# Loading two weight matrices and one V block in halves, summing P times V on DVE, in a decode kernel of one core

## The chip, the cores and the metric

The kernel runs on one core of a Trainium2 chip. The metric is the device time of one execution in microseconds (us), as the median of several runs. TensorE is PE (PEld loads its weights), VectorE is DVE, ScalarE is ACT, GpSimd is POOL; SyncE is SP and issues nearly all DMAs.

## The reference

Two branches over the same input x (2 batches, one position, D = 1024) are mixed by a gate. Branch A is attention with one new query per batch over a cache of 16,384 positions in 32 heads of 128; branch B is an MLP mixer with four weight matrices. All in bfloat16:

```python
x = A_x
g = _sigmoid((x * gate_w).sum(-1, keepdims=True))
# A:
q = (x @ wq).reshape(B, Sq, H, Dh).transpose(0, 2, 1, 3)
scores = jnp.einsum("bhqd,bhkd->bhqk", q, k_cache) * (Dh ** -0.5)
p = _softmax(scores, axis=-1)
o = jnp.einsum("bhqk,bhkd->bhqd", p, v_cache)
a = o.transpose(0, 2, 1, 3).reshape(B, Sq, H * Dh) @ wo
# B: (the shifts of h by positions give zeros, as there is one position)
h = _gelu(_layernorm(x) @ w1);  x1 = x + shifted(h) @ w2
b = x1 + _gelu(_layernorm(x1) @ w3) @ w4
out = g * a + (1 - g) * b
```

K and V are 268 MB each; w3 and w4 7.3 MB each, wq and wo 8.4 MB each, w1 and w2 2.1 MB each. Every byte is used once.

## The kernel before, in words

The work is cut into 32 units. A unit u is a pair of heads (hp, 16 of them) and a batch b; its K and its V are 8.4 MB each, 64 KB to a partition. SBUF holds one large buffer, `mem`, of five cells of 32 KB a partition. K takes cells 0 and 1 in even units, 1 and 2 in odd ones; V takes cells 3 and 4, but the last unit but one has its V in cells 0 and 1. Before the units, cells 3 and 4 hold wq, then w3, then w4, one after the other, and cell 2 holds w1 and w2. So what SP may load next is set by who still reads the cells.

All loads go through SP's queue, in the order of the program; an issue that has to wait holds all that stand behind it. The order before: wq, x, gate_w, w1, w2, K0, w3 (once the q projection has read wq), K1, the first four heads of wo, w4 (`LinearT.load`, L210, once the w3 matmuls have read w3), K2, V0 (`load_v`, L100, once the w4 matmuls have read w4), and then in turn K and V.

In unit n, `score_first` transposes four of eight chunks of K on DVE (L425, two buffers `KT`) and multiplies them on PE with the query (L431). This frees the cell that the next K needs, and `load_k(n + 1)` (L97) is issued. `score_second` does the other four. `softmax_a` and `softmax_b` take the maximum of all scores (the product of `Dm`, L462; DVE's `nb`, L468), the exponentials on ACT (L470) and the sum of their rows (L481, L483). `pv(n - 2)` multiplies the exponentials of two units earlier with their V (L503) into an `oacc` of 128 rows by four blocks of 128 columns; then `load_v(n - 1)` is issued. `pv_end(n - 2)` brings the sum: `pv_sum` copies `oacc` with a scale on ACT (L516), four fp32 products with columns of the selecting matrix `sel8` (L521) add up the blocks, and DVE scales the result by the gate into `OT` (L533). After the second batch of a pair `wo_project` adds the pair's output to two rows of 512 columns, `arow` (L404), in two column groups of PE.

In units 0 and 1 the MLP fills the place of `pv`: `lin3.compute` in unit 0 (a quarter of the w3 matmuls, `softmax_b`, the other three quarters, all at L217), `lin4.compute` in unit 1 in the same way, then `mlp_post4`, which writes branch B into `arow` (L379). wo comes in tiles of four heads (`load_wo`, L397, one buffer).

In the last unit V comes in eleven pieces (`PIECES`, L108), so that `pv_last` can follow them: three pieces as in `pv`, the others with V as the stationary operand (L548). wo's last two heads are loaded behind them. Then DVE and ACT each copy one half of the output row (L606, L608), and SP and ACT store them.

Of the kernel before, what the change touches and what calls it, by code (L numbers as in the profile page):

```python
# [10 lines left out]
FP32 = mybir.dt.float32  # L11
BF16 = mybir.dt.bfloat16
ACTF = mybir.ActivationFunctionType
ALU = mybir.AluOpType
# [9 lines left out]
def kernel(  # L24
# [51 lines left out]
    def misc_psum(shape, dtype=FP32):  # L76
        return mps.tile(shape, dtype, tag="misc", name="misc")
# [4 lines left out]
    def region(cell, elements):  # L82
        return mem[:, cell * CELL : cell * CELL + elements]
# [6 lines left out]
    def cache_rows(cache, u):  # L90
        hp, b = units[u]
        return cache[b, 2 * hp : 2 * hp + 2].rearrange("h s d -> (h s) d").rearrange(
            "(p j) d -> p (j d)", p=P
        )
# [4 lines left out]
    def load_v(u):  # L99
        nc.sync.dma_start(out=region(v_cell[u], NJ * Dh), in_=cache_rows(A_v_cache, u))  # L100

    PIECES = [32] * 6 + [16] * 3 + [8] * 2
    assert sum(PIECES) == NJ

    def load_v_pieces(u):
# [33 lines left out]
    for v in range(4):  # L139
# [36 lines left out]
        axis=AX.X,  # L176
        op=ALU.add,
    )
    oacc = [ops.tile([P, 4 * Dh], FP32, name=f"oacc{k}") for k in range(2)]
    for k in range(2):  # L180
        nc.vector.memset(oacc[k][:], 0.0)
# [14 lines left out]

    class LinearT:

        def __init__(self, W, actT, name, cell, offset):
            self.actT = actT  # L200
            K, self.N = W.shape
            self.R = K // P
            self.C = self.N // P
            self.src = W.rearrange("(p r) n -> p (r n)", p=P)
            at = cell * CELL + offset
            self.dst = mem[:, at : at + self.R * self.N]
            self.acc = mlp.tile([P, self.C, B], FP32, name=f"{name}_acc")

        def load(self):
            nc.sync.dma_start(out=self.dst, in_=self.src)  # L210

        def compute(self, c0, c1):
            wc = self.dst.rearrange("p (r n) -> p r n", n=self.N)
            ps = misc_psum([P, c1 - c0, B])
            for c in range(c0, c1):
                for r in range(self.R):
                    nc.tensor.matmul(  # L217
                        ps[:, c - c0, :],
                        lhsT=wc[:, r, :].rearrange("p (m c) -> p c m", c=self.C)[:, c, :],
                        rhs=self.actT[:, r, :],  # L220
                        start=(r == 0),
                        stop=(r == self.R - 1),
                    )
            nc.vector.tensor_copy(out=self.acc[:, c0:c1, :], in_=ps[:])  # L224

    xn1T = mlp.tile([P, KC, B], BF16)
    hT = mlp.tile([P, KC, B], BF16)
# [5 lines left out]

    lin1 = LinearT(B_w1, xn1T, "w1", 2, 0)
    lin2 = LinearT(B_w2, shT, "w2", 2, KC * D)
    lin3 = LinearT(B_w3, xn2T, "w3", 3, 0)
    lin4 = LinearT(B_w4, h2T, "w4", 3, 0)
    lin1.load()
    lin2.load()
    load_k(0)  # L240
# [5 lines left out]
    for h in range(H):  # L246
        for r in range(KC):
# [4 lines left out]
                start=(r == 0),  # L252
                stop=(r == KC - 1),
            )
    lin3.load()
    qT = const.tile([P, H, B], BF16)
    nc.vector.tensor_copy(out=qT[:], in_=qps[:])
    qdps = misc_psum([P, 4, H * B])
# [100 lines left out]
        nc.vector.tensor_tensor(out=x1T[:], in0=lin2.acc[:], in1=xT[:], op=ALU.add)  # L359
        layernorm_T(x1T[:], xn2T[:], "ln2")  # L360

    NH2 = D // 512
    arow_t = [rps.tile([QP * k + B, 512], FP32, name=f"arow{k}") for k in range(NH2)]
    arow = [arow_t[k][QP * k : QP * k + B, :] for k in range(NH2)]

    def mlp_post4():

        omg = mlp.tile([P, B], FP32, name="omg")
        nc.vector.tensor_scalar(
            out=omg[:], in0=g_rep[:], scalar1=-1.0, scalar2=1.0, op0=ALU.mult, op1=ALU.add  # L370
        )
        nc.vector.tensor_tensor(out=bT[:], in0=lin4.acc[:], in1=x1T[:], op=ALU.add)
        nc.vector.tensor_tensor(
            out=bT[:], in0=bT[:], in1=omg[:].unsqueeze(1).to_broadcast([P, KC, B]), op=ALU.mult
        )
        W = 512 // KC
        for k in range(NH2):
            for c in range(KC):
                nc.tensor.matmul(  # L379
                    arow[k].rearrange("b (m c) -> b c m", c=KC)[:, c, :],  # L380
                    lhsT=bT[:, c, :],
                    rhs=ident_f[:, k * W : (k + 1) * W],
                    start=(c == 0),
                    stop=False,
                    skip_group_check=True,
                )

    OT = const.tile([P, H, B], BF16)
    WOH = 4
    wo_view = A_wo.rearrange("(h d) n -> d h n", d=Dh)  # L390
    wo_tiles = {}

    def load_wo(h0, n, step=WOH):
        t = wopool.tile([P, WOH, D], BF16, name="wo")
        for k in range(0, n, step):
            z = min(n, k + step)
            nc.sync.dma_start(out=t[:, k:z, :], in_=wo_view[:, h0 + k : h0 + z, :])  # L397
        for k in range(n):
            wo_tiles[h0 + k] = t[:, k, :]

    def wo_project(hp):
        for h in (2 * hp, 2 * hp + 1):
            for k in range(NH2):
                nc.tensor.matmul(  # L404
                    arow[k],
                    lhsT=OT[:, h, :],
                    rhs=wo_tiles[h][:, k * 512 : (k + 1) * 512],
                    start=False,
                    stop=(h == H - 1),
                    skip_group_check=True,  # L410
                )

    S_tiles = {}
    st_tiles = {}
# [44 lines left out]
    def softmax_b(u):  # L459
# [9 lines left out]
        for e, rows in enumerate(halves):  # L469
# [6 lines left out]
                accum_out=rs[rows],  # L476
            )
        rs_tiles[u] = rs
        tot_ps = misc_psum([P, 2])
        if u < NU - 1:  # L480
            nc.tensor.matmul(tot_ps[:, 0:1], lhsT=lmat[:], rhs=rs[:], start=True, stop=True)  # L481
# [29 lines left out]
    def pv(u):  # L511
        pv_moving(u, 0, NJ // 4, NJ // 4)

    def pv_sum(u, ot, scaled, last):
        osb = ppool.tile([P, 4 * Dh], FP32, name="osb")
        nc.scalar.activation(  # L516
            out=osb[:], in_=oacc[u % 2][:], func=ACTF.Copy,
            scale=rinvs[u % NP][:, 0:1] if scaled else 1.0,
        )
        for k in range(4):  # L520
            nc.tensor.matmul(  # L521
                ot[:],
                lhsT=osb[:, k * Dh : (k + 1) * Dh],
                rhs=sel8[:, k : k + 5 : 4],
                start=(k == 0),
                stop=(last and k == 3),
            )

    def pv_end(u):
        hp, b = units[u]  # L530
        ot = misc_psum([P, 2])
        pv_sum(u, ot, True, True)
        nc.vector.tensor_scalar(  # L533
            out=OT[:, 2 * hp : 2 * hp + 2, b], in0=ot[:], scalar1=g_rep[:, b : b + 1],
            scalar2=None, op0=ALU.mult,
        )
        if b == B - 1:
            wo_project(hp)

    def pv_last(u):  # L540
        hp, b = units[u]
        ot = misc_psum([P, 2])
        moving = sum(PIECES[:3]) // 4
        pv_moving(u, 0, moving, moving)
        pv_sum(u, ot, False, False)
        V = v_view(u)
        for j in range(4 * moving, NJ):
            nc.tensor.matmul(  # L548
                ot[:],
                lhsT=V[:, j, :],  # L550
                rhs=pts[u % NP][:, j // 4, :, j % 4],
                start=False,
                stop=(j == NJ - 1),
            )
        nc.vector.tensor_tensor(
            out=OT[:, 2 * hp : 2 * hp + 2, b], in0=ot[:], in1=rinvs[u % NP][:], op=ALU.mult
        )
        wo_project(hp)

    compute_gate()  # L560
    layernorm_T(xT[:], xn1T[:], "ln1")
    lin1.compute(0, lin1.C)
    mlp_post1()
    lin2.compute(0, lin2.C)
    mlp_post2()

    for n in range(NU):
        score_first(n)
        if n + 1 < NU:
            load_k(n + 1)  # L570
        else:
            load_v(NU - 2)
        score_second(n)
        softmax_a(n)
        if n == 0:
            lin3.compute(0, FC // 4)
            softmax_b(n)
            lin3.compute(FC // 4, FC)
            gelu_T(lin3.acc[:], h2T[:], FC)
            load_wo(0, WOH)  # L580
            lin4.load()
        elif n == 1:
            lin4.compute(0, KC // 4)
            softmax_b(n)
            lin4.compute(KC // 4, KC)
            mlp_post4()
            load_v(0)
        else:
            pv(n - 2)
            if n < NU - 1:  # L590
                load_v(n - 1)
            else:
                load_v_pieces(NU - 1)
            pv_end(n - 2)
            if n == NU - 1:
                load_wo(H - 2, 2, 1)
            softmax_b(n)
        if n % 4 == 1 and n > 1:
            load_wo(n - 1, min(WOH, H - 2 - (n - 1)))
    pv(NU - 2)  # L600
    pv_end(NU - 2)
    pv_last(NU - 1)

    out_row = mlp.tile([QP + B, 512], BF16)
    rows = out.rearrange("b s d -> (b s) d")
    nc.vector.tensor_copy(out=out_row[0:B, :], in_=arow[0])  # L606
    nc.sync.dma_start(out=rows[:, 0:512], in_=out_row[0:B, :])
    nc.scalar.activation(out=out_row[QP : QP + B, :], in_=arow[1], func=ACTF.Copy)  # L608
    nc.scalar.dma_start(out=rows[:, 512:1024], in_=out_row[QP : QP + B, :])


# [28 lines left out]
```

## Time and profile before

| | |
|---|---|
| median of 3 runs | 1347.13 us (1347.13 to 1348.85) |
| the profiled execution | 1348.32 us; its span, from the first to the last instruction, 1346.6 us |
| mean granted TensorE clock | 0.781 |
| busy: PE, PEld, DVE, ACT, POOL | 790.9, 367.0, 644.4, 127.1, 15.2 us |
| DMA | 573.33 MB, 426 GB/s over the span |
| packets of SP's queue | 16052, 572.54 MB |
| first and last K landing of the units (transposes of unit 3 and unit 31 start) | 177.26 and 1281.67 us |

Times in the profile are microseconds from the start of the span. A line of the timeline gives the start, the time it took, the engine, the line of the kernel, the operation, what it writes and reads, how many instructions it merges, and, in brackets, how long the engine had been idle and what ended that. "SPq L97" is a DMA issue by SP from line 97. A window's line gives the busy time of each engine with the number of instructions, the granted clock, the share of 16 DMA engines in use, and GB/s.

### The profile page before, as it was taken

To read this page: it belongs to the slowest core of one execution; us is meant where nothing else is said; L and a number is where in the kernel's file an instruction comes from. 1 tells how busy PE (TensorE), PEld (TensorE's weight loads), DVE (VectorE), ACT (ScalarE), POOL (GpSimd) and SP (SyncE) were. 2 spreads that over 40 slices of the span, in tenths; PEclk is the share of its full clock that TensorE was granted. 3 is DMA by queue.
4 is the path that set the end of the run, shared out by engine and by line. 5 is a ranking of instruction groups with operands and counts; after the bars stand their busy time and mean duration, and the time that the engine had idled before them with its cause. 6 is when DMAs were issued, how large, how long until landed. Compare 5 with 4: busy or idle time off the path is not lost.

```text
span 1346.6 us, 12381 instructions
## 1 busy us (share of the span) xinstructions
PE 790.9 (59%) x5542; PEld 367.0 (27%) x5542; DVE 644.4 (48%) x503; ACT 127.1 (9%) x197; POOL 15.2 (1%) x54
## 2 busy tenths in 40 slices
PE   2678765554766545566555556655456664555665
PEld 2455322222222222222222222222222222222222
DVE  0434555444555534455554345555344555444450
ACT  0010101111110011110011111001111100111110
POOL 1000000000000000000000000000000000000000
PEclk9967877777887667888777788777778876777886
DMA  9988999999999999999999999999999999999997
GB/s 406 432 368 387 435 436 427 425 429 437 433 431 433 428 439 435 433 433 425 433 433 435 435 435 435 435 432 426 437 437 425 429 433 437 433 433 429 435 435 303
DMA packets 16109, 573.33 MB, mean 426 GB/s; under 512 B 1844, under 2 KB 1848, under 8 KB 6584
## 3 DMA queue, kind: packets, MB, share of 16 engines
q1 hardware_dynamic: 16052, 572.54, 98.8%
q8 instruction: 43, 0.70, 0.2%
q14 instruction: 10, 0.08, 0.0%
q10 hardware_dynamic: 4, 0.00, 0.0%
HBM read 572.53 MB, written 0.00 MB: 425 GB/s over the span
## 4 chain that ended last, share of the span: by engine, by line
DMA 66%; PE 16%; DVE 12%; issue 4%; ACT 0%; another core or an unknown queue 0%; POOL 0%; SPq 0%; DVEq 0%; ACTq 0%
DMA mem<-in_A_k_cache_dram 62%; PE S L431 12%; DVE KT L425 12%; DMA mem<-in_A_v_cache_dram 3%; PE misc L217 3%; DMA xin<-in_A_x_dram 2%; PE misc L248 1%; ACT pt L470 0%; PE arow L379 0%; PE oacc L503 0%; POOL ln_rstd L329 0%; PE misc L462 0%; PE arow L404 0%; PE misc L481 0%
## 5 line engine op out<-in xcount | busy, mean ns | idle before, releaser
L431 PE MATMUL S<-KT,qw 128*128 128x512 bf16 x2048 | 547.9, 418 | 388.4 <-DVE KT L425 388.2
L425 DVE STREAM_TRANSPOSE KT<-mem 128x2048 f32<-128x2048 f32 x256 | 570.8, 2282 | 297.3 <-DMA mem<-in_A_k_cache_dram 245.8
L431 PEld LDWEIGHTS <-qw 128*128 128x128 bf16 x2048 | 219.0, 107 | 712.2 <-issue 533.8
L503 PE MATMUL oacc<-mem,pt 128*8 128x512 bf16 x2008 | 116.9, 386 | 8.7 <-DMA mem<-in_A_v_cache_dram 8.7
L456 ACT ACTIVATE Dm<-ident_s,m 128x128 f32<-128x128 f32 x32 | 12.9, 402 | 1018.4 <-DVE m L454 1018.4
L470 ACT ACTIVATE pt<-St,nb 64x256 bf16<-64x256 f32 x64 | 89.7, 1401 | 58.4 <-DVE nb L468 57.5
L533 DVE TENSOR_SCALAR OT<-misc,g_rep 128x2 bf16<-128x2 f32 x31 | 6.9, 222 | 143.5 <-PE misc L521 143.5
L481 PE MATMUL misc<-rs,lmat 128*128 128x1 f32 x62 | 18.2, 362 | 90.0 <-ACT pt L470 90.0
L503 PEld LDWEIGHTS <-pt 128*8 128x8 bf16 x2008 | 46.7, 87 | 75.7 <-issue 25.3
L452 DVE STREAM_TRANSPOSE St<-S 128x512 f32<-128x512 f32 x32 | 22.9, 717 | 66.2 <-PE S L431 66.2
L483 DVE RECIPROCAL rinv<-misc 128x1 f32<-128x1 f32 x31 | 5.2, 169 | 102.2 <-PE misc L481 102.2
L521 PE MATMUL misc<-sel,osb 128*128 128x2 f32 x256 | 33.7, 254 | 27.1 <-ACT osb L516 27.1
L481 PEld LDWEIGHTS misc<-rs,lmat 128*128 128x128 f32 x62 | 15.5, 311 | 101.2 <-ACT pt L470 101.2
L521 PEld LDWEIGHTS misc<-sel,osb 128*128 128x128 f32 x256 | 31.0, 191 | 43.3 <-ACT osb L516 43.3
L217 PEld LDWEIGHTS <-mem 128*128 128x128 bf16 x576 | 36.3, 170 | 1.8 <-issue 1.4
L470 ACT ACTIVATION_READ_ACCUMULATOR pt<-St,nb 64x1 f32 x64 | 30.5, 477 | 0.0
L516 ACT ACTIVATE osb<-oacc,rinv 128x512 f32<-128x512 f32 x31 | 21.3, 687 | 72.6 <-PE oacc L503 72.6
L248 PE MATMUL misc<-xT,mem 128*128 128x2 bf16 x256 | 7.1, 165 | 26.1 <-DVE xT L243 23.3
L280 POOL TENSOR_TENSOR qw<-qd,mask 128x16 bf16<-128x16 bf16 x32 | 8.4, 265 | 1195.2 <-PE S L431 1166.6
L468 DVE TENSOR_REDUCE nb<-misc 64x1 f32<-64x64 f32 x64 | 14.2, 222 | 5.3 <-PE misc L462 1.3
L224 DVE COPY w_acc<-misc 128x16 f32<-128x16 f32 (+4 forms) x6 | 1.1, 176 | 31.4 <-PE misc L217 31.4
L462 PE MATMUL misc<-Dm,ones_f 128*128 128x128 f32 x64 | 15.8, 331 | 0.0
(83 smaller groups left out, 124.3 us busy)
## 6 DMA issues: line engine op xcount, KB each, us to landing
mem<-in_B_w_dram SPq DMA_DIRECT2D x2, 7168.0 KB, 29.1
wo<-in_A_wo_dram SPq DMA_DIRECT2D x7, 1024.0 KB, 33.0
mem<-in_A_v_cache_dram SPq DMA_DIRECT2D x6, 1024.0 KB, 24.1
mem<-in_B_w_dram SPq DMA_DIRECT2D x2, 2048.0 KB
mem<-in_A_v_cache_dram SPq DMA_DIRECT2D x3, 512.0 KB, 16.7
mem<-in_A_k_cache_dram SPq DMA_DIRECT2D x32, 28.3
wo<-in_A_wo_dram SPq DMA_DIRECT2D x1, 512.0 KB, 32.0
mem<-in_A_v_cache_dram SPq DMA_DIRECT2D x2, 256.0 KB, 13.3
```

The source lines that it names most:

```text
L217: nc.tensor.matmul(ps[:, c - c0, :], lhsT=wc[:, r, :].rearrange("p (m c) -> p c m", c=self.C)[:, c, :], rhs=self.actT[:, r, :], start=(r = ...
L248: nc.tensor.matmul(qps[:, h, :], lhsT=wq_t[:, r, h * Dh : (h + 1) * Dh], rhs=xT[:, r, :], start=(r == 0), stop=(r == KC - 1),)
L425: nc.vector.transpose(out=kt[:], in_=Kc.rearrange("p j d -> p (j d)").bitcast(FP32))
L431: nc.tensor.matmul(S, lhsT=t[:, v, NG - 1 - m : NG - 1 - m + P], rhs=ktb[:, half * GT : (half + 1) * GT, w, :, e], start=(first and n == 0 ...
L452: nc.vector.transpose(out=st[:].rearrange("p j r -> p (j r)"), in_=S[:])
L462: nc.tensor.matmul(R_ps[:], lhsT=ones_f[:], rhs=Dm[:], start=True, stop=True)
L468: nc.vector.tensor_reduce(out=nb[rows], in_=R_ps[rows, rows], axis=AX.X, op=ALU.min)
L470: nc.scalar.activation(out=Pt[rows, :, e, :].rearrange("p (m a) k -> p a k m", a=GT // 4), in_=st[rows, :, 0:NG].rearrange("p (a k) m -> p ...
L481: nc.tensor.matmul(tot_ps[:, 0:1], lhsT=lmat[:], rhs=rs[:], start=True, stop=True)
L503: nc.tensor.matmul(acc[QP * q : QP * q + 8, :], lhsT=pts[u % NP][:, g].rearrange("p h k -> p (h k)"), rhs=v_view(u)[:, 4 * g : 4 * g + 4, ...
L516: nc.scalar.activation(out=osb[:], in_=oacc[u % 2][:], func=ACTF.Copy, scale=rinvs[u % NP][:, 0:1] if scaled else 1.0,)
L521: nc.tensor.matmul(ot[:], lhsT=osb[:, k * Dh : (k + 1) * Dh], rhs=sel8[:, k : k + 5 : 4], start=(k == 0), stop=(last and k == 3),)
```

## The change

- w3, w4 and V0 are loaded in two halves each. The half k of w3 and w4 (four of eight rows of w3 to a partition, 14 of 28 of w4) goes to the start of cell 3 + k; V0's halves are the cells 3 and 4 themselves. `compute(k, c0, c1)` multiplies one half, and the second half is added to the first by DVE. The loads stand right behind the matmuls that free their cells.
- `softmax_b` is cut: the sum of the rows becomes `softmax_c`. In units 0 and 1 `softmax_b` stands in the middle of the first half's matmuls and `softmax_c` behind them.
- `pv_sum` is gone. `pv_rows` adds the four blocks of `oacc` on DVE with a mask that holds the scale and the gate; one or two fp32 products with `hsel` and two small copies give `OT`.
- `arow` is one tile of four rows groups of 256 columns at partitions 0, 32, 64 and 96, for four column groups of PE, in `mlp_post4` as in `wo_project`.
- wo is loaded by pairs of head pairs, with two neighbouring rows to a partition (4 KB runs instead of 2 KB), for 28 heads. The last four heads come as four loads of 2 KB runs behind the last V, and both last pairs are projected at the end; before, two heads came in unit 29 and two behind the last V.
- V of the last unit comes in nine pieces, seven of 32 rows and two of 16, instead of six of 32, three of 16 and two of 8.
- Four tiny loads follow `load_v` in each of units 28, 29 and 30: k rows of 10 + k elements for k of 1 to 10, 12 and 14, from gate_w into tiles that nothing reads.
- At the end DVE and ACT each convert one half of the columns of all rows, and the two batches are stored by SP and ACT.

```diff
+    def load_v_half(u, k):
+        at = slice(k * CELL, (k + 1) * CELL)
+        nc.sync.dma_start(out=region(v_cell[u], NJ * Dh)[:, at], in_=cache_rows(A_v_cache, u)[:, at])
-    PIECES = [32] * 6 + [16] * 3 + [8] * 2
+    PIECES = [32] * 7 + [16] * 2
...
+            self.at = [(cell + k) * CELL + offset for k in range(nparts)]
...
+        def load(self, k=0):
+            n = self.rows * self.N
+            nc.sync.dma_start(out=self.part(k), in_=self.src[:, k * n : (k + 1) * n])
+            if k == 0:
+                nc.vector.tensor_copy(out=acc, in_=ps[:])
+            else:
+                nc.vector.tensor_tensor(out=acc, in0=acc, in1=ps[:], op=ALU.add)
...
+    wo_pairs = A_wo.rearrange("(hp p r) n -> p hp (r n)", p=P, r=2)
+    def load_wo_last():
+        t = wo_tile(HP - LASTP)
+        for k in range(2):
+            for r in range(2):
+                nc.sync.dma_start(out=t[:, k, r, :], in_=wo_heads[:, H - 4 + 2 * k + r, :])
     def wo_project(hp):
+        for r in range(2):
+            for k in range(Q4):
                 nc.tensor.matmul(
                     arow[k],
+                    lhsT=OT[:, hp, r, :],
+                    rhs=wo_tiles[hp, r][:, k * NQ : (k + 1) * NQ],
...
+    probe_sets = {NU - 4: (2, 3, 4, 5), NU - 3: (6, 7, 8, 10), NU - 2: (12, 14, 1, 9)}
+    def load_probes(n):
+        for k in probe_sets.get(n, ()):
+            t = const.tile([k, 32], BF16, name=f"probe{k}")
+            w = 10 + k
+            nc.sync.dma_start(
+                out=t[:, 0:w], in_=gate_w[0 : k * 64].rearrange("(p f) -> p f", p=k)[:, 0:w]
+            )
...
+    def pv_rows(u, mask):
+        nc.vector.tensor_scalar(
+            out=part[:], in0=acc[:, 0:Dh], scalar1=mask[:, 0:1], scalar2=None, op0=ALU.mult
+        )
+        for k in range(1, 4):
+            in0 = acc[:, k * Dh : (k + 1) * Dh]
+            twice = k == 3
+            nc.vector.scalar_tensor_tensor(
+                out=red[:] if twice else part[:],
...
         if n == 0:
-            lin3.compute(0, FC // 4)
+            load_wo_pair(0)
+            lin3.compute(0, 0, FC // 2)
             softmax_b(n)
-            lin3.compute(FC // 4, FC)
+            lin3.compute(0, FC // 2, FC)
+            lin4.load(0)
+            softmax_c(n)
+            lin3.compute(1, 0, FC)
+            lin4.load(1)
             gelu_T(lin3.acc[:], h2T[:], FC)
-            load_wo(0, WOH)
-            lin4.load()
         elif n == 1:
-            lin4.compute(0, KC // 4)
+            lin4.compute(0, 0, KC // 2)
             softmax_b(n)
-            lin4.compute(KC // 4, KC)
+            lin4.compute(0, KC // 2, KC)
+            load_v_half(0, 0)
+            softmax_c(n)
+            lin4.compute(1, 0, KC)
+            load_v_half(0, 1)
             mlp_post4()
-            load_v(0)
         else:
             pv(n - 2)
             if n < NU - 1:
                 load_v(n - 1)
+                load_probes(n)
```

## The prediction

> **What bounds the kernel now.** I read the page's slices first, then the stream of transfers in the stretches where the slices sag, then the queue SP in the order of time, and last a middle unit and the tail. The slices (40 of 33.7 us each):
>
> ```profile
> DMA  9988999999999999999999999999999999999997
> GB/s 406 432 368 387 435 436 427 425 429 437 433 431 433 428 439 435 433 433 425 433 433 435 435 435 435 435 432 426 437 437 425 429 433 437 433 433 429 435 435 303
> ```
>
> DMA is full from end to end; no compute engine is over 59% busy. Over 177 to 1281 us the windows give 433 GB/s: that is the ceiling of this kernel, and 573 MB must pass under it. So time is lost only where transfers stop: slices 3 and 4 (368, 387) and the last one (303). The third view cuts the first of these stretches into windows (columns: start and end, length, busy time of PE, PEld, DVE, ACT, POOL, granted clock, DMA share, GB/s):
>
> ```profile
> 75.00:89.00 14.00, 10.76 (x157) 10.46 (x156) 1.92 (x6) 3.21 (x5) 0.27 (x1) 0.62 0.95 405
> 89.00:98.00 9.00, 5.00 (x77) 4.80 (x76) 3.76 (x8) 0.25 (x1) 0.00 (x0) 0.50 0.70 258
> 98.00:112.00 14.00, 12.91 (x48) 5.05 (x47) 12.53 (x6) 0.00 (x0) 0.00 (x0) 0.85 0.94 406
> 112.00:131.00 19.00, 15.19 (x190) 12.62 (x189) 4.56 (x8) 3.21 (x5) 0.27 (x1) 0.69 1.02 440
> 131.00:139.00 8.00, 7.32 (x93) 6.49 (x92) 4.41 (x5) 0.00 (x0) 0.00 (x0) 0.50 0.64 231
> 139.00:155.00 16.00, 13.88 (x59) 5.68 (x58) 13.80 (x7) 0.00 (x0) 0.00 (x0) 0.98 0.96 414
> ```
>
> There are two holes, about 89 to 98 and 131 to 139. A window counts a packet where it starts, so edges blur; the whole stretch does not: 5670+2322+5684+8360+1848+6624 = 30.5 MB in 80 us, where 433 GB/s would move 34.6 MB. The missing 4.1 MB are 9.5 us. The timeline of the same stretch tells why:
>
> ```profile
> 82.99 10.77 PE L217 MATMUL misc<-xn2T,mem 128*128 128x2 bf16 x168
> ...
> 93.78 0.33 SPq L210 DMA_DIRECT2D mem<-in_B_w_dram  x1
> ...
> 134.51 0.33 SPq L100 DMA_DIRECT2D mem<-in_A_v_cache_dram  x1
> ```
>
> w4 goes to the bytes of w3, so SP holds it (and the K load queued behind it) until the last w3 matmul ends at 93.8; the queue, with only K1 and wo in it, has run dry at about 91.7. V0 goes to the bytes of w4, is issued when the w4 matmuls end at 134.5, and K2 had ended near 132. Each time about 1 us passes from issue to first packet, and the first packets after a pause are slow: 64 KB packets take 3.2 to 3.5 us in the packet records of 135 us, 2.42 us elsewhere. In the middle no hole is to be had:
>
> ```profile
> 1136.37 0.33 SPq L97 DMA_DIRECT2D mem<-in_A_k_cache_dram  x1
> ...
> 1150.66 0.33 SPq L100 DMA_DIRECT2D mem<-in_A_v_cache_dram  x1
> ...
> 1164.34 4.50 DVE L425 STREAM_TRANSPOSE KT<-mem 128x2048 f32<-128x2048 f32 x2 [7.52 <-DMA mem<-in_A_k_cache_dram]
> ...
> 1174.85 0.33 SPq L97 DMA_DIRECT2D mem<-in_A_k_cache_dram  x1
> ```
>
> A unit (K's landing at 1125.5 to that at 1164.3) is 38.8 us, two loads of 19.4. V is issued 13.7 us before the K load ahead of it lands, K some 9 us before the V load ahead of it ends (1164.3 + 19.4 against 1174.9). DVE waits 7.5 us for K.
>
> **The change, part by part.**
>
> *Halves of w3 and w4 (the first hole).* w4's first half needs only the first half of the w3 matmuls: 56 (3.65 us in the trace, 75.0 to 78.6), the fp32 product of Dm (to 79.3), 56 more (168 take 10.77, so 3.6): 82.9. At 82.9 the queue still holds K1 and wo until 91.7, so SP issues 9 us ahead. The row sum's product moves behind these 56 matmuls, where exp has ended (82.5): the 3.3 us that PE stood before it are filled, and the last 112 matmuls (7.2 us) end at 90.7 instead of 93.8. w4's second half is issued there, 10 us before the first half (3.67 MB, 8.5 us) has passed. K2 follows the scores of unit 1, which start 3 us earlier with the gelu: issue near 103 instead of 105.9, with w4 running to 109. Closed.
>
> *Halves of V0 (the second hole).* The scores of unit 1 end near 113.6. 56 + 56 matmuls on w4's first half, again with the softmax between: about 121, and V0's first half is issued while K2 runs to 128.4. The other 112 end at 129, and V0's second half is issued while the first (9.7 us) runs to 138. Then the MLP row: 32 matmuls of 32 columns in place of 16 of 64, fp32 in two passes, so 64 records for 32; at the 97 ns each of L379 (3.11 us for 32) 6.2 us, at best unchanged. PE is free at 133 to 136, the four score chunks take 7.2 us as at 138.2 to 145.4, K3 is issued by 143; V0 runs to 147.7. Cover 4.7 us; without it the price is about that shortfall. Closed.
>
> Together at most 9.5 us. Part of the sag is not a hole (wo's 2 KB packets, instruction loads), and a DMA engine that lags today catches up in the holes: the last engines were busy to about 91.7 where the mean stopped at 90.4. By packets, the engine that ends last idles 3.3 and 3.7 us and has two slow packets of 1.1 and 1.0: 9.1. If the two starts stayed slow, 7.0. I take 9.0, less 0.5 for lag that is no longer absorbed (0 to 1.4): 8.5.
>
> *wo by pairs.* Same bytes, 4 KB runs for 28 of 32 heads instead of 2 KB. Seven units with a 1 MB wo load take 41.2 against 38.7 us, 2.46 us for 1.05 MB, where 433 GB/s need 2.42: 0.04 x 7 = 0.3 us at least. Packet records give more (84 ns for 2 KB, 159 for 4 KB, 16 engines: 1.0 us in all), but overlap. I take 0.3, range 0 to 1.0.
>
> *DVE sums.* Out go, per unit, one ACT copy (0.69), eight PE records (1.05) and one DVE scaling (0.22). In come one scaling of 128x4 (0.2), three passes over 128 and one over 256 columns from PSUM, half of the PE records (0.5) and two small copies (0.4). No row shows such a pass: L533 with 2 columns costs 0.22, L606 with 512 costs 0.68, so 0.3 for 128 and 0.45 for 256: 1.35 us. The chain goes from 1.96 to about 2.4 us, DVE gains 1.5 us a unit (some 48 us of busy time). All of it lies in the 7.5 us that DVE waits for K, behind the issue of V; behind it queue only the softmax's nb and the next transposes. Cost 0; without the cover 0.5 to 1.5 us a unit, 15 to 45 us in all.
>
> *The tiny loads.* Four go into SP's queue behind V27, V28 and V29. SP needs 0.41 to 0.46 us for such an issue (L123, L125), 1.8 us for four, and its next issue (K, 24 us later in the unit above) waits anyway. In the stream: x and gate_w (4 and 2 KB, 128 rows each) land together within 0.3 us after wq, in which their 384 packets passed. Twelve loads with 81 rows by that row: 0.06 us by packets, 1.8 by loads at 0.15. Nobody reads them. I take 0.1.
>
> A rule speaks against all the splitting. The Trainium skill, page "DMA: Bandwidth & Descriptors", section "Anatomy of one DMA", puts some 2.0 us of fixed cost on each transfer; with twelve tiny ones and three added halves that is an estimate of 30 us, and a sum that says slower. The row above, 0.3 us for two loads queued behind another, says that this cost is latency and is not paid in a full queue.
>
> *The tail.* First windows, then the timeline:
>
> ```profile
> 1336.00:1338.00 2.00, 1.08 (x34) 1.00 (x35) 0.00 (x0) 0.00 (x0) 0.00 (x0) 0.50 0.63 256
> 1338.00:1340.00 2.00, 1.10 (x32) 0.94 (x32) 0.00 (x0) 0.00 (x0) 0.00 (x0) 0.50 0.57 223
> ```
>
> ```profile
> 1342.33 1.20 PE L404 MATMUL arow<-wo,OT 128*2 128x512 bf16 x4 [0.25 <-DVE OT L555]
> ...
> 1343.56 0.68 DVE L606 CAST out_row<-arow 2x512 bf16<-2x512 f32 x1 [1.29 <-PE arow L404]
> ```
>
> From 1336 only about 9 of 16 DMA engines still work: some lag by 5 us, and the last bytes are wo's. The change has the same bytes, now 1 MB of wo behind V; the slow engines' end stays. After the last wo block: before, two matmuls of 512 columns (0.63) and a copy of 512 columns (0.68). After, if PE takes the blocks as they land, four of 256 columns in four column groups, about 0.4 (0 saved if all sixteen wait for the last), then 128 columns on DVE and 128 on ACT, 0.3 to 0.4. I take 0.5 saved, 0 to 1.2. Two larger last V pieces (16 rows in place of 8) lie before wo's end: 0, and their packets save 0.1.
>
> Sum: 8.5 + 0.3 + 0.5 + 0.1 - 0.1 = 9.3 us. The profiled execution took 1348.3 us (span 1346.6, 1.7 around it), which gives 1339.0; the runs' median 1347.13 lies 1.2 lower, and against it the forecast is 1337.8.
>
> **Rivals.**
>
> *One hole stays.* If the MLP row costs clearly over 6 us or PE comes late to unit 2, K3 misses its 4.7 us: half of 8.5 is lost, 1342. For: PE ran at a clock of 0.50 there. Against: DVE, not PE, paces the chunks.
>
> *The halves free nothing early.* If a half's bytes are held until the whole matrix has been read, both holes stay; only the filled PE wait and the tail remain: 1346 to 1347. Against: K loads are already released by halves of a tile today (L97 goes after four of eight chunks).
>
> *Slower: the tiny loads hold SP.* In the page's queue view SP waited 28.2 us at the V pieces (L108) for earlier V loads whose bytes they don't touch, so an issue can wait for an older transfer to land. If a tiny load waits so for the load in front of it, the next K comes after the queue is empty; it decides once that K is over 9 us late. A restart costs about 4.5 us as in the two holes, so 13.5 us for three units: 1351. Against: those waits came with eight loads in flight, and here at most three are older and not landed.
>
> **How the numbers follow.** Forecast 0.82, one hole 0.06, nothing freed 0.05, tiny loads hold SP 0.07. The forecast's own ends: 1347.1 - (9.5 + 1.0 + 1.2 + 0.1) = 1335.3 and 1347.1 - (7.0 - 1.4 - 1.8) = 1343.3; two runs of before differ by 1.7 us, so I open the low end to 1334, and close the high one at 1342.5, since its parts would all have to go wrong together. A measurement of this kernel tells about 0.2% (2.7 us) from no change. Faster: 0.82 and 0.06, 0.88. Same: most of the third case, 0.04. Slower 0.08.
>
> **What would show it.** Right: from 75 to 150 us about 430 GB/s throughout, w4's first half issued near 83, V0's near 121, transposes of unit 3 near 168 instead of 177.3, and every later landing of K as much earlier; units of 38.7 us as before, DVE's busy time up by some 50 us. Wrong: a window under 350 GB/s between 75 and 150, longer units with DVE at K's landing still in pv_end, or SP standing at a tiny load past 1170 us with the windows after it dipping.

## The result, and the profile after

The changed kernel takes 1341.34 us (median of 4 runs, 1341.19 to 1341.40) against 1347.13 us; the ratio is 0.9952, with a 95% interval from 0.9936 to 0.9967. It is faster by 5.8 us; 9.3 had been forecast. The two profiled executions, 1348.32 and 1341.31 us, lie 7.0 us apart. The kernel before scatters (1346.4 to 1348.9 us over all 37 of its runs in this study), the changed one hardly does.

The slices of the page, of the changed kernel:

```profile
DMA  9999999999999999999999999999999999999997
GB/s 406 425 429 434 438 435 431 435 420 444 425 435 437 435 427 435 423 435 435 437 433 429 427 435 427 425 435 432 437 437 429 425 431 435 425 435 433 433 427 306
```

Slices 3 and 4, 368 and 387 GB/s before, are at 429 and 434. The same windows as before, and the whole stretch in one:

```profile
89.00:98.00 9.00, 4.99 (x33) 2.67 (x33) 5.66 (x8) 0.25 (x1) 0.00 (x0) 0.51 1.05 446
131.00:139.00 8.00, 7.05 (x48) 3.29 (x43) 7.68 (x5) 0.00 (x0) 0.00 (x0) 0.94 1.01 432
75.00:155.00 80.00, 66.96 (x670) 43.69 (x669) 45.61 (x52) 7.41 (x13) 0.79 (x3) 0.81 1.01 432
```

Both holes are gone: 258 and 231 GB/s became 446 and 432, and the stretch runs at the ceiling. The issues in the timeline of the changed kernel (x2 merges the two halves; a row spans from the first to the last):

```profile
83.02 7.85 SPq L226 DMA_DIRECT2D mem<-in_B_w_dram  x2
...
102.58 0.33 SPq L97 DMA_DIRECT2D mem<-in_A_k_cache_dram  x1
...
120.89 7.75 SPq L104 DMA_DIRECT2D mem<-in_A_v_cache_dram  x2
...
138.31 0.33 SPq L97 DMA_DIRECT2D mem<-in_A_k_cache_dram  x1
```

w4's first half is issued 10.8 us earlier than w4 before, V0's first half 13.6 us earlier than V0, and K3 7.1 us earlier. The chain of waits shows the first transposes of units 3, 14 and 15 (after the K load that releases each), in the kernel before and then in the changed one:

```profile
177.26 2.32 DVE KT L425
...
609.53 2.32 DVE KT L425
...
650.72 2.32 DVE KT L425
```

```profile
169.18 2.32 DVE KT L472
...
601.63 2.32 DVE KT L472
...
642.87 2.32 DVE KT L472
```

The lead is 8.08 us at unit 3 and 7.90 at unit 14, but 7.85 at unit 15, behind a unit with a wo load. Six such units lie between unit 3 and unit 31; they last 41.25 to 41.34 us, against 41.17 to 41.26 before. The tail gives back more; first the end of the kernel before, then that of the changed one:

```profile
1343.60 0.59 ACT L608 ACTIVATE out_row<-arow 2x512 bf16<-2x512 f32 x1 [11.79 <-PE arow L404]
1344.21 0.53 ACTq L609 DMA_DIRECT2D out_dram<-out_row  x1
1344.27 0.33 SPq L607 DMA_DIRECT2D out_dram<-out_row  x1
```

```profile
1335.62 0.38 PE L441 MATMUL arow<-wo,OT 128*2 128x256 bf16 x4 [0.26 <-DMA wo<-in_A_wo_dram]
...
1336.06 0.29 DVE L688 CAST out_row<-arow 98x128 bf16<-98x128 f32 x1 [2.27 <-PE arow L441]
1336.38 0.28 ACT L689 ACTIVATE out_row<-arow 98x128 bf16<-98x128 f32 x1 [33.01 <-DVE out_row L688]
1336.68 0.63 SPq L691 DMA_DIRECT2D out_dram<-out_row  x1
1336.69 1.37 ACTq L691 DMA_DIRECT2D out_dram<-out_row  x1
```

PE takes wo's blocks as they land. But ACT's copy waits for DVE's ("<-DVE out_row"; before, the two copies ran side by side, from 1343.56 and 1343.60), and ACT needs 1.37 us for the issue of its four-row store, where the two-row store before took 0.53.

### The profile page after: what moved, and what is told of

The parts are those of the page before. It is cut to its first block, busy times and chain, and to the rows that moved or that the text cites. A ratio compares the mean times of both kernels' runs of the same rounds, so it can differ in the third digit from the quotient of the medians.

```text
span 1339.6 us, 12506 instructions
## 1 busy us (share of the span) xinstructions
PE 770.4 (58%) x5502; PEld 351.5 (26%) x5502; DVE 705.6 (53%) x695; ACT 105.1 (8%) x165; POOL 15.2 (1%) x54
## 4 chain that ended last, share of the span: by engine, by line
DMA 67%; PE 16%; DVE 12%; issue 4%; ACT 0%; another core or an unknown queue 0%; POOL 0%; SPq 0%; DVEq 0%; ACTq 0%
DMA mem<-in_A_k_cache_dram 62%; PE S L478 13%; DVE KT L472 12%; PE misc L233 2%; DMA mem<-in_A_v_cache_dram 2%; DMA xin<-in_A_x_dram 2%; DMA wo<-in_A_wo_dram 1%; PE misc L268 1%; ACT pt L517 0%; PE arow L402 0%; PE oacc L553 0%; DVE St L499 0%; POOL ln_rstd L350 0%; PE misc L344 0%
## 5 line engine op out<-in xcount | busy, mean ns | idle before, releaser
L569 DVE TENSOR_SCALAR part<-oacc,maskr 128x128 f32<-128x128 f32 x31 | 10.9, 351 | 82.7 <-PE oacc L553 82.7
L600 PE MATMUL misc<-hsel,red 128*128 128x2 f32 x112 | 17.1, 257 | 51.5 <-DVE red L575 51.5
L600 PEld LDWEIGHTS misc<-hsel,red 128*128 128x128 f32 x112 | 15.5, 198 | 64.8 <-issue 62.6
L575 DVE SCALAR_TENSOR_TENSOR part<-oacc,maskr,part 128x128 f32<-128x128 f32 x62 | 21.8, 351 | 2.2
L609 DVE CAST OT<-misc 64x2 bf16<-64x2 f32 x56 | 9.0, 160 | 22.5 <-PE misc L600 22.2
L515 DVE TENSOR_REDUCE nb<-misc 64x1 f32<-64x64 f32 x64 | 14.2, 222 | 4.9 <-PE misc L509 3.1
```

Source lines behind the costliest of these rows:

```text
L515: nc.vector.tensor_reduce(out=nb[rows], in_=R_ps[rows, rows], axis=AX.X, op=ALU.min)
L575: nc.vector.scalar_tensor_tensor(out=red[:] if twice else part[:], in0=in0.unsqueeze(1).to_broadcast([P, 2, Dh]) if twice else in0, scalar ...
L600: nc.tensor.matmul(ot[:, r, :], lhsT=red[:, r : 2 * Dh : 2], rhs=hsel[:], start=True, stop=True,)
```

## The experiments

They ran in three groups, each on one chip and in turn with the kernel before: no_tiny, halves_alone, no_halves and wo_2k_runs (the kernel before: 1348.38); aligned_wo, halves_shifted, split_store and tiny_ten (1348.69); v0_whole, halves_dve_sums, best and best_mem (1347.53). The changed kernel itself ran in none of them; no_tiny stands for it in the first. So a difference of a few tenths between groups counts only where the profiles show it too. Medians are in us.

| kernel | median | what it is |
|---|---|---|
| no_tiny | 1341.23 | changed, without the tiny loads |
| halves_alone | 1339.79 | before, with the halves and the cut softmax |
| no_halves | 1348.36 | changed, w3, w4 and V0 whole, the softmax uncut |
| v0_whole | 1343.05 | changed, V0 alone whole |
| wo_2k_runs | 1342.36 | changed, wo in 2 KB runs |
| aligned_wo | 1340.10 | changed, wo at byte 0 of 256 |
| halves_shifted | 1341.83 | halves_alone, wo at byte 64 of 256 |
| halves_dve_sums | 1339.77 | halves_alone, sums on DVE |
| split_store | 1340.74 | changed, other copies and stores |
| tiny_ten | 1355.58 | changed, ten tiny loads in three units |
| best | 1339.82 | no_tiny, aligned_wo and split_store |
| best_mem | 1337.01 | best, the large buffer at byte 0 of 256 |

The theory at the start: the closed holes are the whole gain, and the missing part went to wo's loads and to the store. The rivals: the tiny loads or the DVE sums cost it, or the rest of the change brings a part of the gain.

### Which part brings the gain

**halves_alone**

```diff
-    lin3 = LinearT(B_w3, xn2T, "w3", 3, 0)
+    lin3 = LinearT(B_w3, xn2T, "w3", 3, 0, 2)
...
+            load_v_half(0, 0)
```

> The kernel before with the halves of w3, w4 and V0 and the cut softmax alone; wo, the sums, the output row and the last V pieces as before. My theory: the whole gain is the two closed holes. Transposes of unit 3 start near 169.2 as in the changed kernel (177.3 before), wo units last 41.18 us, the last store takes 0.6 us less than in the changed kernel, so this kernel is faster than the changed one by 0.5 to 1.5 us: about 1340. Rival: the new tail and wo loads bring a part of the gain, and this kernel is slower than the changed one, 1342 to 1343.

Measured: 1339.79 us, ratio 0.9936 (0.9924 to 0.9949), 1.55 us faster than the changed kernel (1.44 faster than no_tiny in its own group). Unit 3 starts at 168.96. The halves, together with the cut softmax, are the whole gain, and the rest of the change takes some of it back.

**no_halves**

```diff
-    lin3 = LinearT(B_w3, xn2T, "w3", 3, 0, 2)
+    lin3 = LinearT(B_w3, xn2T, "w3", 3, 0)
...
-            load_v_half(0, 0)
-            load_v_half(0, 1)
+            load_v(0)
```

> The changed kernel with w3, w4 and V0 loaded whole as before and the softmax uncut; all else as changed. My theory: both holes are back, and what remains of the change costs some 0.5 to 1 us: 1347.5 to 1348.5, transposes of unit 3 at 177 us. Rival: the rest of the change brings 0.5 us or more: 1346.5 or less.

Measured: 1348.36 us against 1348.38 for the kernel before in the same group, ratio 1.000 (0.9991 to 1.0009). Both holes are back: the windows 89 to 98 and 131 to 139 move 276 and 264 GB/s. Unit 3 starts at 176.24, 1.0 us sooner than before; the wo units (41.26 to 41.46 us) and the tail give that back.

**v0_whole**

```diff
-            load_v_half(0, 0)
-            load_v_half(0, 1)
             mlp_post4()
+            load_v(0)
```

> The changed kernel with V0 loaded whole behind the last w4 matmul, as before; w3 and w4 still in halves. It weighs the two holes apart. In the prediction the first is worth about 4.5 to 5 us and the second 4 to 4.5. With V0 whole its issue comes at about 128.4 us, when K2 (to about 128) is just done: I expect a shorter hole than before, since all came 6 us sooner but K2's end too, 2 to 4 us late at the start of unit 3, so 171 to 173 us instead of 169.2, and 1343.3 to 1345 in all. Rival: closing the first hole moves PE so far ahead that V0 whole comes in time: 1341.3.

Measured: 1343.05 us, just under the range expected; unit 3 starts at 171.12, 6.1 us sooner than before. Of these, 1.0 us is there in no_halves too, without any half, so the halves of w3 and w4, with the cut softmax, are worth 5.1 us (176.24 - 171.12), and those of V0 1.9 us more (171.12 - 169.18), once the first hole is closed. V0 whole is issued just as K2 ends, 6.0 us sooner than before, and a narrower hole remains there:

```profile
128.54 0.33 SPq L100 DMA_DIRECT2D mem<-in_A_v_cache_dram  x1
```

```profile
120.00:128.00 8.00, 7.91 (x127) 7.83 (x127) 0.62 (x3) 1.15 (x2) 0.00 (x0) 0.50 0.75 322
128.00:132.00 4.00, 3.32 (x74) 3.13 (x73) 3.38 (x5) 0.00 (x0) 0.00 (x0) 0.50 0.80 266
```

(the first fence is SP's timeline, the second the windows of v0_whole: 322 and 266 GB/s around that issue).

### The tiny loads

**no_tiny**

```diff
                 load_v(n - 1)
-                load_probes(n)
```

> The changed kernel without its twelve tiny loads. My theory: they cost nothing, since they queue behind a V load that SP has already issued and nobody reads them. Time within 0.3 us of the changed kernel (1341.3), landings of K in units 28 to 31 within 0.2 us. Rival: they are where a part of the missing gain went (12 issues and 12 landings late in the run): then 1339.5 to 1340.5.

Measured: 1341.23 us. They cost 0.1 us, which is within the runs' scatter, and the rival falls.

**tiny_ten**

```diff
-    probe_sets = {NU - 4: (2, 3, 4, 5), NU - 3: (6, 7, 8, 10), NU - 2: (12, 14, 1, 9)}
+    probe_sets = {n: tuple(range(2, 12)) for n in (NU - 4, NU - 3, NU - 2)}
```

> The changed kernel with ten tiny loads (2 to 11 rows) in place of four in each of units 28, 29 and 30. It tests the prediction's slower rival: an issue waits for the landing of the load eight places before it in SP's order (in the kernel before SP stood 14.2 us at the V pieces for V30, eight loads back). With four, that load has always landed. With ten, the ninth and tenth wait for the first two tiny ones, which lie behind a V load of 8.4 MB: SP is held until V has landed and the next K is issued 7 to 9 us late, on an empty queue. I expect SP to stand some 30 us in each of the three units, units longer by about 4.5 us each: 1354 (1350 to 1357). If the tiny loads never hold SP whatever their number: 1341 to 1342.

Measured: 1355.58 us, 14.2 us more than the changed kernel, which is 4.7 us for each of the three units. The timeline of SP, and SP's waits in that stretch (waiting line and what it waited for; us in total, times, longest):

```profile
1182.19 0.33 SPq L100 DMA_DIRECT2D mem<-in_A_v_cache_dram  x1
1182.57 33.11 SPq L456 DMA_DIRECT2D probe<-in_gate_w_dram  x10
...
1195.34 20.33 SPq L456 DMA_DIRECT2D probe<-in_gate_w_dram  x4
...
1215.77 0.36 SPq L97 DMA_DIRECT2D mem<-in_A_k_cache_dram  x1
```

```profile
SPq L456 <- DMA mem<-in_A_v_cache_dram: 57.8, 3, 19.5
SPq L456 <- DMA mem<-in_A_k_cache_dram: 43.4, 3, 16.5
```

SP stands 33 us among the tiny loads (the row of 1195.34 is the last four of the ten, from a narrower window). Six go out at once; the seventh goes at 1195.34, when K has landed, and the eighth at 1214.67, when V has: each waits for the load eight places before it. The expectation had the ninth and the tenth wait, for the first two tiny loads; SP is stopped before it comes to them. The K load behind them goes out at 1215.77 instead of 1206.70, and the window 1212 to 1216 moves 0 GB/s:

```profile
1212.00:1216.00 4.00, 3.41 (x16) 1.40 (x15) 2.78 (x2) 0.00 (x0) 0.00 (x0) 1.00 0.01 0
```

The prediction's slower rival exists, with its price; with ten tiny loads a unit it decides, with the change's four it does not (no_tiny, 0.1 us).

### wo's loads

**wo_2k_runs**

```diff
-            out=t[:].rearrange("p k r n -> p k (r n)"), in_=wo_pairs[:, hp0 : hp0 + 2, :]
+            out=t[:].rearrange("p k r n -> p (k r) n"), in_=wo_heads[:, 2 * hp0 : 2 * hp0 + 4, :]
```

> The changed kernel with all of wo in runs of 2 KB by heads, as before, in place of 4 KB runs by neighbouring rows (one fp32 product a unit in place of two goes with it). In the two profiles a unit with a wo load takes 41.27 us with 4 KB runs and 41.18 with 2 KB. My theory: that difference is the runs'; wo units go back to 41.18, 0.5 to 0.7 us in all, about 1340.7. Rival (the prediction's term): longer runs are cheaper, and this kernel is slower by 0.3 to 1.0 us; or the 0.09 us come from something else and nothing moves.

Measured: 1342.36 us, 1.0 us slower (1.1 against no_tiny), and wo units of 41.39 to 41.46 us. My theory fell: longer runs do save. But halves_alone loads the same 2 KB runs and has wo units of 41.17 to 41.18 us (one of 41.48). The two differ in the address of the wo tile, which lies behind small tiles that the change adds: byte 64 of a 256-byte block in the changed kernel, byte 0 before. These places are counted from the sizes and the order of the tiles; no trace shows an address.

**aligned_wo**

```diff
+    pad_t = const.tile([P, 96], BF16, name="pad")
+    nc.vector.memset(pad_t[:], 0.0)
     neg_half = const.tile([P, 1], FP32)
```

> The changed kernel with one unused tile of 192 bytes a partition put ahead, which moves the wo tile (and all later ones) from byte 64 of a 256-byte block to byte 0, where it lay in the kernel before. What it is about: with 2 KB runs the wo units last 41.42 us in wo_2k_runs and 41.17 in halves_alone, from equal loads; the one difference that I found is the place of the tile, and 2 KB packets take 87.6 ns against 84.5 (nine in ten under 93 against 84). My theory: a shifted destination slows some DMA engines' short packets. 4 KB packets fall from 162.5 to about 160 ns, wo units from 41.27 to 41.1 to 41.2, seven of them 0.6 to 1.1 us: about 1340.4. Rival: the DVE sums or the PE order slow the loads; then nothing moves (1341.3).

Measured: 1340.10 us, 1.24 us faster than the changed kernel (the profiled spans, 1338.5 and 1339.6 us, differ by 1.1). wo units fall to 41.11 to 41.15 us. With the tile at byte 0, then, 4 KB runs are 0.03 us a unit shorter than the 2 KB runs of halves_alone; at byte 64 they are 0.15 us shorter (41.26 against 41.41).

**halves_shifted**

```diff
+    pad_t = const.tile([P, 32], BF16, name="pad")
+    nc.vector.memset(pad_t[:], 0.0)
     neg_half = const.tile([P, 1], FP32)
```

> The kernel halves_alone with one unused tile of 64 bytes a partition, so that wo lies at byte 64 of a 256-byte block as in the changed kernel; nothing else differs. My theory: 2 KB packets go to 87 to 88 ns, wo units from 41.17 to about 41.4, seven of them 1.5 to 1.8 us: 1341.3 to 1341.6. Rival (the place does not matter): 1339.8, units 41.17.

Measured: 1341.83 us, 2.04 us slower than halves_alone (2.1 in the profiled spans), wo units of 41.39 to 41.41 us. Both ways the place of the tile moves the time. The pad shifts all later tiles, not wo alone; that wo's loads are what slows is seen in their packets:

| packets of wo | byte 0 of 256 | byte 64 of 256 |
|---|---|---|
| 2 KB: mean, nine in ten under | 84.5, 84 ns (halves_alone) | 87.1, 93 ns (halves_shifted) |
| 4 KB: mean, nine in ten under | 159.7, 159 ns (aligned_wo) | 162.5, 167 ns (changed kernel) |

**best_mem**

```diff
+    pada_t = const.tile([P, 64], BF16, name="pada")
+    nc.vector.memset(pada_t[:], 0.0)
     mem = const.tile([P, 5 * CELL], BF16, name="mem")
```

> As best, with the large buffer of K, V and the weights moved from byte 128 to byte 0 of a 256-byte block by an unused tile of 128 bytes. If the place matters for long runs as it does for wo's: the 64 KB packets fall below their 2420 ns and 8 KB ones below 313, 0.3 to 3 us in all. If only short runs feel it, as I expect: within 0.3 us of best, 8 KB packets in the tail 2 to 6 ns shorter.

Measured: 1337.01 us, ratio 0.9922 (0.9909 to 0.9934): 2.8 us faster than best, the fastest kernel of the study. My expectation was wrong. The large buffer lay at byte 128 of a 256-byte block in all other kernels. In the middle of the run (177 to 1281 us), 48% of the 64 KB packets of best take 2418 ns or less, and nine in ten 2426 or less; of best_mem's, 98% take 2418 or less. The slow packets count here, not the mean: the kernel before has a mean of 2423.3 ns against best's 2426.2, the same 2426 for nine in ten, and units as long as best's. The gain itself is seen in the units: between units 3 and 31, the 22 without a wo load take 856.0 us together in best and 854.3 in best_mem. The lead over best grows from 0.7 us at unit 3 to 2.6 at unit 31.

### The sums and the store

**halves_dve_sums**

```diff
-        pv_sum(u, ot, True, True)
+        red = pv_rows(u, mask)
+        nc.tensor.matmul(ot[:], lhsT=red[:, 0:Dh], rhs=hsel[:], start=True, stop=True)
```

> halves_alone with the sums of P times V on DVE in place of ACT and four products, the wo tile kept at byte 0 of a 256-byte block by an unused tile. The prediction put this part at 0, under DVE's wait of 7.5 us for K. My theory: DVE busy rises by 45 to 65 us and the time stays within 0.3 us of halves_alone (1339.8). Rival: 1.3 us more in the chain behind the last V pieces shows at the end, where PE follows the pieces: 1340.3 to 1341.

Measured: 1339.77 us, the same as halves_alone (and so are the profiled spans, 1338.1 and 1338.2 us), with DVE busy for 700.7 us instead of 644.4.

**split_store**

```diff
-    nc.vector.tensor_copy(out=out_row[used, 0:half], in_=arow_t[used, 0:half])
-    nc.scalar.activation(out=out_row[used, half:NQ], in_=arow_t[used, half:NQ], func=ACTF.Copy)
+    nc.vector.tensor_copy(out=out_row[lo, :], in_=arow_t[0][lo, :])
+    nc.scalar.activation(out=out_row[hi, :], in_=arow_t[1][hi, :], func=ACTF.Copy)
+    for k, queue in ((0, nc.sync), (2, nc.scalar), (1, nc.sync), (3, nc.sync)):
```

> The changed kernel with the output rows in two PSUM tiles (two column groups each), copied side by side by DVE and ACT, and stored by four two-row stores, three on SP and one on ACT, in place of two four-row stores. In the profiles the end of the last wo product to the end of the span is 3.6 us in the changed kernel (copies one after the other 0.60, ACT's issue 1.37) and 2.9 in halves_alone. My theory: 0.2 us from the copies and 0.3 to 0.4 from the issues, about 1340.8. Rival: the write to HBM is what takes the time, and nothing or under 0.2 us moves.

Measured: 1340.74 us, 0.6 us faster than the changed kernel. The timeline of split_store:

```profile
1335.82 0.42 DVE L689 CAST out_row<-arow 34x256 bf16<-34x256 f32 x1 [2.26 <-PE arow L442]
1335.86 0.38 ACT L690 ACTIVATE out_row<-arow 34x256 bf16<-34x256 f32 x1 [32.49 <-PE arow L442]
1336.27 0.94 SPq L692 DMA_DIRECT2D out_dram<-out_row  x3
1336.27 0.60 ACTq L692 DMA_DIRECT2D out_dram<-out_row  x1
```

The copies run side by side, and three stores on SP and one on ACT take 0.94 and 0.60 us to issue. From the last product's end to the span's end it is 3.3 us instead of 3.6. The last product itself starts 0.2 us sooner; how that and the rest of the 0.6 us come about, this run does not tell.

**best**

```diff
-                load_probes(n)
...
+    pad_t = const.tile([P, 96], BF16, name="pad")
```

> The changed kernel without the tiny loads, with wo at byte 0 of a 256-byte block (aligned_wo) and the four two-row stores (split_store). If the gains of the two add: 1341.3 - 1.2 - 0.6 = 1339.5. If the store's gain is hidden by the later landing of wo: 1340.

Measured: 1339.82 us. The two gains add up to 1.5 of 1.8 us; what is missing is about the size of the runs' scatter.

## Why the prediction was right, and where its sizes were off

The direction and the mechanism held: the closed holes are the gain. The range held with 1.2 us to spare. The prediction closed its upper end at 1342.5 instead of 1343.3, since its parts "would all have to go wrong together"; three of them, wo, the tail and the base, did miss in the same direction, so that this end held was partly luck. Term by term:

- **The holes: 8.5 forecast, 8.1 measured** at unit 3. w4's first half was forecast for 82.9 and went at 83.0, though in another order: the first 56 w3 matmuls ran among the score chunks (65.9 to 71.2), and the scores ended 2.2 us later. V0's first half was forecast for 121 and went at 120.9; K2 near 103, at 102.6. K3 came at 138.3 instead of 143: the MLP row was charged with up to 6.2 us, by 97 ns a record, and its 64 records take 2.87 us at the same granted clock of 0.50. Halving the columns halved the record's price; the rival of one remaining hole lost its ground there. The two holes are not equal: 5.1 and 1.9 us, and 1.0 that no_halves has without them, where some 4.5 each were read from the windows. (One reading of them was narrow: the sixteen first packets after the pause at 134.5 took 2.8 to 3.5 us, not 3.2 to 3.5.) Closing the first one also brings the MLP forward (V0 whole goes at 128.54 instead of 134.51), and so narrows the second.
- **wo by pairs: 0.3 gained forecast, 0.6 lost** between units 3 and 31 (six units with a wo load longer by 0.06 to 0.09 us each, 0.5 together, the others by 0.1 in all, when the 1.2 us of the two heads that the kernel before loaded in unit 29 are set aside; the prediction counted seven, but the first wo load lies in unit 0, ahead of these). The step that failed is "same bytes, 4 KB runs": it took the runs for the only thing that changes. The runs do save: with the tile at byte 0 some 0.03 us a unit, the prediction's 0.04, and at byte 64 about 1.0 us in all (wo_2k_runs). But the tiles that the change adds push the wo tile to byte 64 of a 256-byte block, and that costs 1.1 to 1.2 us (aligned_wo). No step of the prediction looked at addresses.
- **The tail: 0.5 gained forecast, 0.3 lost.** From the start of the last wo product to the span's end it was 3.7 us before (1342.94 to 1346.6) and is 4.0 (1335.62 to 1339.6). PE does take the blocks as they land, in 0.38 us. The failed step is "128 columns on DVE and 128 on ACT, 0.3 to 0.4": both read one PSUM tile and run one after the other, 0.60; with a PSUM tile, and rows, of its own for each they run side by side (split_store). And the store's issue was charged with nothing, as it had been there before; its four rows cost ACT 0.84 us more than two did before.
- **The DVE sums: 0 forecast, 0 measured** (halves_dve_sums). Single passes take 0.35 and 0.48 us where 0.3 and 0.45 were estimated; DVE's busy time rose by 56 us there, and by 61 in the changed kernel, where some 48 were forecast.
- **The tiny loads: 0.1 forecast, 0.1 measured.** The Trainium skill's 2.0 us of fixed cost (page "DMA: Bandwidth & Descriptors", section "Anatomy of one DMA") would by estimate have made 24 us of these twelve. That section gives the figure for transfers issued from GpSimd, while these go out on SP, and it puts most of it down to the wait for the last byte's confirmation, not to the transfer's place in a queue. Behind other loads in a full queue, the twelve cost nothing that can be measured.
- **The base.** 8.1 - 0.6 - 0.3 is 7.2 us, and the profiled executions differ by 7.0. The remaining 1.2 us are a step of the sum: every term was read from an execution of 1348.3 us, and the gain was then taken off a median of 1347.1 from three runs. In the three groups, the median of the kernel before was 1348.38, 1348.69 and 1347.53. Why it scatters and the changed kernel does not, no run here settles.

The uneven end of the DMA engines, taken over from before, is there in halves_alone, the changed kernel, best and best_mem alike: 237 GB/s in the changed kernel from 1330 to 1332 us, 205 in best_mem from 1328 to 1330. Its cause stays open; the addresses are not all of it.

## What to carry to other kernels

In a kernel at the ceiling of its transfers, look for the slices where the queue runs dry, and ask which instruction the next load waits for: a buffer that is released by halves is worth about what the hole is wide, and less where an earlier hole's end has already moved its load forward. No other part of this change gained. Price a change also for what it moves without naming it, such as the addresses of tiles that are allocated later and a copy that now shares a PSUM tile with another engine's. Extra loads were free here while few were in flight, and dear once an issue has to wait for an old one to land.

## What was not expected of the hardware

- **The place of a destination inside a 256-byte block.** At byte 64, the slow packets of wo take 8 to 9 ns more (93 against 84 ns for 2 KB, 167 against 159 for 4 KB); at byte 128, the slow 64 KB packets take 8 ns more (2426 against 2418). The extra is about the same for each packet whatever its size: 10% for 2 KB, 0.3% for 64 KB. Even so the place of the large buffer is worth 2.8 us here, as nearly all the time is transfers. The Trainium skill, page "DMA: Bandwidth & Descriptors", section "How a descriptor splits into AXI transactions", says that when a descriptor does not start at a multiple of 256 bytes, its first transaction starts at the boundary below and fetches bytes that are not used. By that rule, as an estimate, a run of 2, 4 or 64 KB takes one transaction more, whatever its length. An extra of fixed size agrees with that, but the section speaks of reads, and what is seen here is the place of the destination. Why only a part of the packets pays it (half of the 2 KB ones stay at 85 ns) is open.
- **An issue that waits for the load eight places before it.** SP stood 33 us in tiny_ten, at tiny loads that share no byte with the loads they waited for: the seventh for K, the eighth for V. Each time that the queue ran dry for it cost 4.7 us.
- **The issue of a small store.** Four rows of 512 bytes, 32 partitions apart, kept ACT for 1.37 us and SP for 0.63; two neighbouring rows of 1 KB kept them 0.53 and 0.33, and two neighbouring rows of 512 bytes kept ACT 0.60 (split_store) and 0.53 (best). Whether the number of the rows or their distance makes the price, no run here tells.
